# Top-2 routing of the first batch in two pieces: an mLSTM, MoE and dense layer kernel on one core

## The chip, the cores and the metric

The kernel runs on one core of a Trainium2 chip. Its time is the device time of one execution in microseconds. Before the change the median of three runs is 506.29 us (506.05 to 507.14).

The core has five engines that run their own instruction queues in order: PE (TensorE, matmuls and transposes), DVE (VectorE), ACT (ScalarE), POOL (GpSimd) and SP (SyncE, which here only starts DMAs). They wait for each other by semaphores. SBUF is the working memory, and PSUM is the memory that PE writes to and that DVE and ACT can read and write.

## The reference

Three layers stand one behind the other, all in float32. The first is an mLSTM over 2 batches, 8 heads, 768 positions and 40 values a head. The second sends each of the 1536 tokens to two of eight experts. The third is dense with a cosine gate.

```python
# mLSTM, for each position t
m_new = np.maximum(f_gate[:, :, t] + m, i_gate[:, :, t])
C = f_stab * C + i_stab * outer(vt, kt);  n = f_stab * n + i_stab * kt
y[:, :, t] = sigmoid(o_gate[:, :, t]) * (C @ qt) / max(abs(n @ qt), 1)
# mixture of experts, x has 1536 rows of 320
logits = x @ w_gate
noisy_logits = logits + np.log1p(np.exp(x @ w_noise)) * noise
top2 = np.argpartition(-noisy_logits, 2, axis=1)[:, :2]
top2_w = softmax of the two noisy logits
out[mask] += top2_w[mask, k, None] * (np.maximum(x[mask] @ w1[e], 0.0) @ w2[e])
# dense layer
h = x @ w_in;  out = (h * np.cos(h)) @ w_out
```

## The kernel before

**Attention steps.** The mLSTM is computed in chunks of 128 positions: chunks 0 to 5 are the first batch (b = 0), 6 to 11 the second. `att_step(n)` (L857) is one step of a pipeline over the chunks. In step n, `mm_out(n)` computes the output of chunk n on PE, while `mm_s(n + 2)` makes the scores of a later chunk, `mk_w` (ACT's exponentials with POOL's masks) makes its decay weights, and `mk_p(n + 1)` (DVE, into `ppt`) multiplies the two. `mk_e` makes the exponentials for the state (`get`), `mk_q` the scaled queries (`qtt`), `mm_state` and `mk_state` the state. `mk_y(n)` (L326) turns the output of chunk n into the rows x(n): an Abs on ACT and four instructions on DVE, the last of which is L338 and writes `xt`. `tanh_o` (L151) prepares the output gates of two chunks in a tile `ogt`.

**Router.** x(n) is transposed on PE by `rt_a(n)` (L352, copy on ACT into `xTt`) and multiplied with the router's weights by `rt_b(n)` (L361, copy on ACT into `Lt`, called Lt(n) below); both run one step later, in step n + 1. When all six chunks of a batch are there, `router_a0` and `router_a1` make the noisy logits and their top 2 (`r_mx`, `r_ix`), `router_a2` the one-hot rows `r_os`, `router_b` the place of every token in its expert's list (`pp` and `jj` hold place and block), `router_b1` and `router_b2` one-hot matrices of these (`r_am`, `r_bm`), and `router_c` on PE and `router_d` on DVE the list of tokens, by which POOL's indirect DMAs gather rows. `router_a3` and `router_a4` make the softmax of the two weights, which is used only when the expert outputs are combined.

**What sets the order.** Instructions stand in each engine's queue in the order in which the code calls them. Around the fixed body of `att_step`, tables insert further calls: `inner[n, w]` inside mm_out(n) after head pair w, `mid[n]` before rt_b(n - 1), `fill[n]` before mk_y(n), and `put(n, ...)` at the end of step n. After attention, `expert_step` runs 64 times (two steps begin inside attention), and `put(k, ...)` with the same k adds work to expert step k. Experts' weights are split by ACT and POOL or DVE into `wh` and `wl`.

**Buffers.** A tile gets one buffer of a ring when it is made, and the first instruction that writes to it waits until all instructions on the buffer's former tile are done. PSUM has rings of four (`psA`), three (`psS`) and one (`psM`). rt_b, router_b and router_c use the single `psM`. mm_state(n) and mm_out(n) each take a tile of `psS` in every step with a state, and rt_a takes its tile from there in steps 7 and 9, otherwise from `psM`. In batch 0, `pp` and `jj` lie in SBUF; in batch 1 they lie in the PSUM tile of router_b.

**Around the change.** In step 6 (L928 to L931) ACT changes its function table, because Ln is not in the one used until then, and the whole top 2 of batch 0 is made; tanh_o(5) stands at the end of step 5, the last place where the old table holds. router_a4(0) stands at the end of step 9, in spare columns of mm_out(9)'s tile.

Of the kernel before, what the change touches and what calls it, by code (L numbers as in the profile page):

```python
# [14 lines left out]
U32 = mybir.dt.uint32  # L15
AF = mybir.ActivationFunctionType
OP = mybir.AluOpType
# [5 lines left out]
NC = S // C  # L23
DM = H * D
E = 8
# [16 lines left out]
def tile_mlstm_moe_moe2(ctx, tc, qk, kv, og, gt, wcat, noise, wm1, wm2, cst, out):  # L42
    nc = tc.nc
    V, A, G, T, Y = nc.vector, nc.scalar, nc.gpsimd, nc.tensor, nc.sync
# [13 lines left out]
    def psS():  # L58
        return ps.tile([128, 512], FT, name="pS", tag="S", bufs=3)

    def psM():
        return ps.tile([128, 512], FT, name="pM", tag="M", bufs=1)
# [65 lines left out]
    for i in range(NB):  # L128
        t = ap_.tile([128, 3, NH, C], FT, name=f"qk{i}")
# [4 lines left out]
    for i in range(2):  # L134
        t = ap_.tile([128, H, 64], FT, name=f"kb{i}")
        G.memset(t, 0.0)
        KBS.append(t)
    for i in range(2):
        t = ap_.tile([128, NH, 82], FT, name=f"st{i}")
# [14 lines left out]
    L = [{} for _ in range(2 * NC)]  # L154
# [189 lines left out]
    nz = cp.tile([128, B * NC, E], FT, name="nz")  # L344
    R = [dict() for _ in range(B)]

    def cols(x, n, k):

        c0 = min(128 * k, DM - 128)
        return x[:n, c0:c0 + 128]  # L350

    def rt_a(n, ps_=None):  # L352
        b, c = divmod(n, NC)
        d = L[n]
        p = (ps_ or psM)()
        for k in range(3):
            T.transpose(p[:, 128 * k:128 * k + 128], cols(d["x"], 128, k), ident)
        d["xT"] = ap_.tile([128, 3, 128], FT, name="xTt", bufs=2)
        A.activation(d["xT"], p[:, :KW].rearrange("p (k t) -> p k t", t=128), AF.Copy)

    def rt_b(n, ps_=None):  # L361
        b, c = divmod(n, NC)
        d = L[n]
        p = (ps_ or psM)()
        for k in range(3):
            T.matmul(p[:, :128], d["xT"][:, k, :], wc[:, k:k + 1, :].to_broadcast([128, 8, 16]),  # L366
                     start=(k == 0), stop=(k == 2))
        if c == 0:
            R[b]["L"] = mp.tile([128, NC, 16], FT, name="Lt", bufs=1)
        A.activation(R[b]["L"][:, c, :], p[:, :16], AF.Copy)  # L370
# [20 lines left out]
    def rsm(shape, name, dt=FT):  # L391
        return mp.tile(shape, dt, name=name, tag=name, bufs=1)
# [2 lines left out]
    rb = rsm([128, B, E], "r_rb", BF)  # L395


    def router_a0(b):
        r = R[b]
        q = r["q"] = psM()  # L400
        t = r["t"] = q[:, 0:48].rearrange("p (c e) -> p c e", e=E)
        A.activation(t, r["L"][:, :, 8:16], AF.Abs)
        A.activation(t, t, AF.Exp, scale=-1.0)
        A.activation(t, t, AF.Ln, bias=1.0)

    def router_a1(b):
        r = R[b]
        t, z, lg = r["t"], r["L"][:, :, 8:16], r["L"][:, :, 0:8]
        V.scalar_tensor_tensor(out=t, in0=z, scalar=0.0, in1=t, op0=OP.max, op1=OP.add)
        V.tensor_tensor(out=t, in0=t, in1=nz[:, b * NC:(b + 1) * NC, :], op=OP.mult)  # L410
        ts = rsm([128, NC, E], "r_t")
        V.tensor_tensor(out=ts, in0=t, in1=lg, op=OP.add)
        mx = rsm([128, NC, 8], "r_mx")
        ix = rsm([128, NC, 8], "r_ix", U32)
        for c in range(NC):
            V.max(out=mx[:, c, :], in_=ts[:, c, :])
        for c in range(NC):
            V.max_index(out=ix[:, c, :], in_max=mx[:, c, :], in_values=ts[:, c, :])
        r["mx"], r["ix"] = mx, ix

    def router_a2(b):
        r = R[b]
# [17 lines left out]
    def router_a4(b, p=None):  # L440
        w = R[b]["w"]
        p = psM() if p is None else p
        e, t = p[:, 352:358], p[:, 360:366]
        A.activation(e, w[:, 1], AF.Exp)
        V.tensor_scalar(t, e, 1.0, 1e-9, op0=OP.add, op1=OP.add)
        V.reciprocal(w[:, 0], t)
        V.tensor_tensor(out=w[:, 1], in0=e, in1=w[:, 0], op=OP.mult)

    def router_b(b):

        r = R[b]
        q = r["q"] = psM()
        v = q[:, 384:384 + NC * E + E]
        T.matmul(v, tri, os_.rearrange("p c e -> p (c e)"), start=True, stop=False)
        T.matmul(v, ones, rb[:, b:b + 1, :].to_broadcast([128, NC + 1, E]), start=False, stop=False)
        for c in range(NC):
            T.matmul(v[:, (c + 1) * E:], ones, os_[:, c:c + 1, :].to_broadcast([128, NC - c, E]),
                     start=False, stop=(c == NC - 1))
        rk = q[:, 0:96].rearrange("p (k c e) -> p k c e", k=2, e=E)
        V.tensor_tensor(out=rk, in0=v[:, 0:NC * E].rearrange("p (c e) -> p c e", e=E)[:, None]  # L460
                        .to_broadcast([128, 2, NC, E]), in1=r["oh"], op=OP.mult)
        rr, y = (q[:, 440 + 12 * i:452 + 12 * i].rearrange("p (k c) -> p k c", c=NC) for i in range(2))
        V.tensor_reduce(rr, rk, axis=AX.X, op=OP.add)
        V.tensor_scalar(y, rr, -63.75, MAGIC7, op0=OP.add, op1=OP.add)
        js = rsm([128, 2, NC], "r_jj")
        jj, pp = ((q[:, 464 + 12 * i:476 + 12 * i].rearrange("p (k c) -> p k c", c=NC) for i in range(2)) if b else
                  (js, rsm([128, 2, NC], "r_pp")))
        V.tensor_scalar(js, y, MAGIC7, 1.0 / C, op0=OP.subtract, op1=OP.mult)
        V.scalar_tensor_tensor(out=pp, in0=js, scalar=-float(C), in1=rr, op0=OP.mult, op1=OP.add)
        if b:  # L470
            V.tensor_scalar(jj, y, MAGIC7, 1.0 / C, op0=OP.subtract, op1=OP.mult)
        r["pp"], r["jj"], r["rr"], r["tot"] = pp, jj, rr, v[:, NC * E:]
        if not b:
            router_p(b)
            router_s(q)

    def router_p(b):
        r = R[b]
        pos = r["pos"] = rsm([128, 2, NC], f"r_pos{b}", U32)
        V.tensor_scalar(pos, r["rr"], float(ROWS - 1 if b else ROW1[0] - 1), None, op0=OP.min)  # L480
        fl = rsm([128, E], "r_fl")
        V.tensor_tensor(out=fl, in0=r["tot"], in1=lims[b], op=OP.is_gt)
        V.tensor_reduce(flag[:, b:b + 1], fl, axis=AX.X, op=OP.max)

    def router_s(q):

        so, t = q[:, 128:136], q[:, 136:144]
        V.tensor_reduce(so, os_[:, 0:NC].rearrange("p c e -> p e c"), axis=AX.X, op=OP.add)
        V.tensor_tensor(out=t, in0=so, in1=joint, op=OP.mult)
        V.tensor_tensor(out=rb[:, 1], in0=t, in1=row1, op=OP.add)  # L490
# [366 lines left out]
    def att_step(n):  # L857
# [11 lines left out]
        def between(w):  # L869
            if n + 2 in ROWS64:  # L870
                if w == 1:
                    rt_a(n - 1)
                    mk_w(n + 2, (0,), False)
            elif w < NH - 2:
                mm_s(n + 2, (w + 1,))
            elif w == NH - 2:
                rt_a(n - 1, psS if n in (7, 9) else None)
            for f, a in inner.pop((n, w), []):
                f(*a)
# [6 lines left out]
        if n:  # L886
            rt_b(n - 1)
# [27 lines left out]
    at, pre, mid, fill, inner = {}, {}, {}, {}, {}  # L915

    def put(k, fn, *a):
        at.setdefault(k, []).append((fn, a))
# [1 line left out]
    def step(k):  # L920
        expert_step(*divmod(k, 8))

    for i in range(1, NC):
        put(i, tanh_o, i)
    for i in range(8):
        put((6, 7, 7, 8, 10, 10, 10, 11)[i], load_w, 0, i, 1)
    put(11, load_w, 1, 0, 2)
    mid[6] = [(A.preload_act_table_set, ("natural_log_exp_and_others",))]  # L928
    fill[6] = [(router_a0, (0,))]
    put(6, router_a1, 0)  # L930
    put(6, router_a2, 0)  # L931
    mid[7] = [(mk_w, (9, (0,), False))]
    fill[7] = [(mk_w, (9, (1,), False)), (mk_m, (9, 0, 1)), (router_b, (0,))]
    put(7, router_a3, 0)
    put(7, router_b1, 0, 0)
# [4 lines left out]
    inner[9, 1] = [(mk_w, (11, (0,), False))]  # L940
    mid[9] = [(mk_w, (11, (1,), False))]
    fill[9] = [(mk_m, (11, 0, 1))]
    put(9, lambda: router_a4(0, L[9]["po"]))
    put(10, split, 0)
    put(10, split, 1)
    inner[11, 0] = [(prep_slot, (0, 0, psA))]
# [6 lines left out]
    for n in range(2 * NC):  # L953
        att_step(n)
        for f, a in at.pop(n, []):
            f(*a)
    rt_a(2 * NC - 1)
    step(1)
    rt_b(2 * NC - 1)
    router_a0(1)  # L960
    router_a1(1)
    att.close()
    wp = ctx.enter_context(tc.tile_pool(name="wp", bufs=1, reuse_waits="tile"))

# [13 lines left out]
    put(7, router_d, 1)  # L978
    put(9, router_a3, 1)
    put(12, router_a4, 1)  # L980
    for i in range(4):
        put(7 + i // 2, gather, 2, i)
        put((13, 14, 15, 15)[i], prep_slot, 2, i, (psA, psM)[i % 2])
# [23 lines left out]
    for f in range(12):  # L1007
        k = 18 + (15 * f) // 4
# [10 lines left out]
    for q in range(3):  # L1019
        for i in range(3):  # L1020
            c = 3 * q + 3 + i
# [25 lines left out]
    with tc.If(over > 0):  # L1047
        WD = [dr.tile([S, E], FT, name=f"wd{b}") for b in range(B)]
        for b in range(B):
            r = R[b]  # L1050
# [6 lines left out]
        for b in range(B):  # L1057
            with tc.For_i(0, NC, 1) as it:
# [4 lines left out]
                p = psM()  # L1063
# [6 lines left out]
                for e in range(E):  # L1070
                    acc = psA()
                    for f in range(8):
                        w = mp.tile([128, FW], FT, name="wr", tag="wh", bufs=4)
                        Y.dma_start(w, wm1[e, :, f, :])
                        p = psS()
                        for k in range(3):
                            r = slice(64 * (k == 2), 128)
# [6 lines left out]
                                           in1=x2[:, :DM], op0=OP.mult, op1=OP.add)  # L1084
                d = {}
# [3 lines left out]
                for f in range(16):  # L1089
                    wh, wl = W2[f // 4][:, 0, f % 4, :], W2[f // 4][:, 1, f % 4, :]  # L1090
                    p = psS()
# [6 lines left out]
                t = mp.tile([128, DM], FT, name="yt", tag="yt", bufs=3)  # L1098
# [81 lines left out]
```

## Time and profile before

| | |
|---|---|
| median of the runs | 506.29 us |
| the profiled execution | 505.76 us |
| its span (first to last instruction) | 504.0 us |
| PE busy | 481.1 us (95%) |
| DVE busy | 353.2 us (70%) |
| ACT busy | 325.6 us (65%) |
| POOL busy | 273.1 us (54%) |
| granted TensorE clock | 0.998 of full speed |

The profile is one execution. The busy time of an engine says how full it is over the whole span; what a step waits for is read from the engines' timelines, where a row carries in brackets the idle time of the engine just before it and the instruction that ended it. Attention steps 5 to 11 take about 42 to 85 us of the span, and the expert steps follow up to about 280 us.

### The profile page before, as it was taken

The numbers are of one execution on the slowest core, as the hardware profiler recorded it, in microseconds if no ns is written. First come the engines' busy times: TensorE is split into PE (matmuls) and PEld (weight loads), VectorE is DVE, ScalarE is ACT, GpSimd is POOL, SyncE is SP. The second block draws the span as 40 slices with busy tenths as digits, with TensorE's granted clock in tenths as the row PEclk, the third lists the DMA queues.
The fourth block names the chain that finished last, engine by engine and source line by source line (L and its number), as shares of the span: only waits on it lengthen the run. The fifth ranks groups of instructions, "written<-read, shape, count | busy, mean of one in ns | idle before, by whom it ended". The sixth has DMA issues, their size and how long they took to land.

```text
span 504.0 us, 9162 instructions
## 1 busy us (share of the span) xinstructions
PE 481.1 (95%) x3295; PEld 466.0 (92%) x3295; DVE 353.2 (70%) x749; ACT 325.6 (65%) x691; POOL 273.1 (54%) x228
## 2 busy tenths in 40 slices
PE   5999889999999999999999989899999999999995
PEld 4998888989999999999999988899999999999995
DVE  4565697874577777787667588589756755787772
ACT  3787856655454545545553765678787787787772
POOL 4654665877558684968587786363364357200000
PEclk9999999999999999999999999999999999999999
DMA  6989754964739274645657373310020012001001
GB/s 200 299 286 295 236 180 144 322 211 152 294 128 322 103 260 176 257 182 188 257 166 263 117 284 100 105 52 1 0 92 29 0 35 84 2 2 39 1 2 45
DMA packets 25429, 74.47 MB, mean 148 GB/s; under 512 B 3840, under 2 KB 11456, under 8 KB 25376
## 3 DMA queue, kind: packets, MB, share of 16 engines
q1 hardware_dynamic: 22784, 65.20, 37.1%
q0 software_dynamic: 2592, 8.61, 5.7%
q8 instruction: 28, 0.46, 0.4%
q14 instruction: 25, 0.20, 0.1%
HBM read 64.57 MB, written 9.22 MB: 146 GB/s over the span
## 4 chain that ended last, share of the span: by engine, by line
PE 79%; DVE 9%; ACT 3%; issue 3%; DMA 2%; POOL 1%; SPq 1%; ACTq 0%; DVEq 0%; POOLq 0%
PE pS L606 34%; PE pA L615 10%; PE pA L611 10%; PE pA L612 10%; PE pS L321 3%; PE pM L567 2%; DMA wraw<-wm 2%; PE pA L262 1%; PE pA L623 1%; PE pA L624 1%; PE pS L317 1%; PE pM L366 1%; PE pA L253 1%; DVE c_t L729 1%; POOL xgt L558 1%
## 5 line engine op out<-in xcount | busy, mean ns | idle before, releaser
L599 POOL TENSOR_TENSOR wl<-wraw,wh 128x704 fp32r<-128x704 f32 x70 | 125.2, 1801 | 59.8 <-ACT wh L597 53.1
L661 DVE SCALAR_TENSOR_TENSOR hb<-pS,hb 128x384 fp32r<-128x384 f32 (+2 forms) x128 | 45.8, 390 | 45.2 <-ACT hb L658 44.5
L597 ACT ACTIVATE wh<-wraw 128x704 fp32r<-128x704 f32 x80 | 62.8, 786 | 15.8 <-PE pA L623 9.3
L606 PE MATMUL pS<-xh,wh 128*128 128x448 f32 (+1 forms) x240 | 69.3, 343 | 0.5 <-ACT xh L569 0.5
L606 PE MATMUL pS<-xh,w 128*128 128x384 f32 x288 | 66.3, 339 | 1.5 <-DVE m_t L770 1.5
L606 PE MATMUL pS<-xh,wl 128*128 128x448 f32 (+1 forms) x240 | 65.9, 329 | 1.0 <-POOL wl L599 1.0
L611 PE MATMUL pA<-wh,hb 128*128 128x320 f32 x208 | 62.3, 309 | 0.0
L612 PE MATMUL pA<-wl,hb 128*128 128x320 f32 x208 | 62.2, 309 | 0.0
L755 ACT ACTIVATE m_t<-pS,magic 128x384 f32<-128x384 f32 x64 | 37.1, 579 | 27.7 <-PE pS L606 27.2
L658 ACT ACTIVATE hb<-pS 128x448 fp32r<-128x448 f32 (+1 forms) x80 | 37.7, 471 | 26.7 <-PE pS L606 19.2
L606 PEld LDWEIGHTS pS<-xh,w 128*128 128x128 f32 x288 | 50.1, 189 | 2.9 <-DVE m_t L770 2.9
L770 DVE SCALAR_TENSOR_TENSOR m_t<-m_t,pS 128x384 f32<-128x384 f32 x64 | 35.4, 553 | 16.9 <-ACT m_t L769 16.3
L615 PE MATMUL pA<-wh,hb 128*128 128x320 f32 x208 | 44.0, 311 | 2.8 <-DVE hb L661 2.6
L606 PEld LDWEIGHTS pS<-xh,wl 128*128 128x128 f32 x240 | 42.8, 189 | 3.6 <-POOL wl L599 1.4
L606 PEld LDWEIGHTS pS<-xh,wh 128*128 128x128 f32 x240 | 40.5, 189 | 1.6 <-ACT xh L569 0.6
L776 POOL TENSOR_TENSOR wl<-m_t,wh 128x384 fp32r<-128x384 f32 x25 | 25.5, 1019 | 30.2 <-ACT wh L774 21.1
L756 DVE TENSOR_SCALAR m_t<-m_t 128x384 f32<-128x384 f32 x64 | 23.1, 361 | 26.4 <-ACT m_t L755 26.2
L606 PE MATMUL pS<-xl,wh 128*128 128x448 f32 (+1 forms) x160 | 39.6, 328 | 0.0
L611 PEld LDWEIGHTS pA<-wh,hb 128*128 128x128 f32 x208 | 38.7, 186 | 0.6
L612 PEld LDWEIGHTS pA<-wl,hb 128*128 128x128 f32 x208 | 38.7, 186 | 0.5
L569 ACT ACTIVATE xh<-pM 128x384 fp32r<-128x384 f32 (+2 forms) x38 | 17.6, 462 | 30.5 <-PE pM L567 30.4
L757 DVE SCALAR_TENSOR_TENSOR m_t<-pS,m_t 128x384 f32<-128x384 f32 x64 | 35.7, 557 | 2.2
(217 smaller groups left out, 1226.7 us busy)
## 6 DMA issues: line engine op xcount, KB each, us to landing
wraw<-wm SPq DMA_DIRECT2D x36, 704.0 KB
raw<-wm SPq DMA_DIRECT2D x16, 704.0 KB
gb<-gd SPq DMA_DIRECT2D x10, 512.0 KB
kv<-kv SPq DMA_DIRECT2D x12, 324.0 KB
qk<-qk SPq DMA_DIRECT2D x24, 160.0 KB
yd<-yt SPq DMA_DIRECT2D x22, 160.0 KB
wraw<-wm SPq DMA_DIRECT2D x8, 352.0 KB
ogt<-og SPq DMA_DIRECT2D x6, 320.0 KB
```

Source lines behind the costliest of these rows:

```text
L597: A.activation(wh, raw[:, f, :], AF.Copy)
L599: eng.tensor_tensor(out=wl, in0=raw[:, f, :], in1=wh.bitcast(FT), op=OP.subtract)
L606: T.matmul(p[:, :n], w[:, 128 * k:128 * k + 128], x[:, m, :], start=(i == 0), stop=(i == 7))
L611: T.matmul(a[:n, :DM], hh[:, s], wh[:, KW:], start=first, stop=False)
L612: T.matmul(a[:n, :DM], hh[:, s], wl[:, KW:], start=False, stop=False)
L615: T.matmul(a[:n, :DM], hl[:, s], wh[:, KW:], start=False, stop=last)
L658: A.activation(hh[:, :n], p[:, :n], AF.Relu)
L661: V.scalar_tensor_tensor(out=hb[:, o:o + z - a], in0=p[:, a:z], scalar=0.0, in1=hh[:, a:z].bitcast(FT), op0=OP.max, op1=OP.subtract)
L755: A.activation(t, m["p"], AF.Identity, bias=magic, scale=0.5 / PI)
L757: V.scalar_tensor_tensor(out=t, in0=m["p"], scalar=0.5 / PI, in1=t, op0=OP.mult, op1=OP.subtract)
L770: V.scalar_tensor_tensor(out=s, in0=s, scalar=1.0, in1=m["p"], op0=OP.subtract, op1=OP.mult)
L776: eng.tensor_tensor(out=m["hl"], in0=m["t"], in1=m["hh"].bitcast(FT), op=OP.subtract)
```

## The change

The top 2 of batch 0 is now made in two pieces. Chunks 0 to 4 go through router_a0 and router_a1 in step 5, and chunk 5 alone in step 6, followed by router_a2 as before. router_a0 now includes the three DVE instructions that were the beginning of router_a1, so these stand where `fill` stands, ahead of mk_y. The scratch columns are taken from the tile of the last rt_b instead of a new `psM` tile. The table load and tanh_o(5) move into mm_out(5) behind head pair 1. `pp` of batch 0 moves from an SBUF tile to columns 384 to 395 of the PSUM tile of rt_a(6) (`L[NC]["pt"]`). router_a4(0) moves to expert step 13 with a `psM` tile.

```diff
     def rt_a(n, ps_=None):
-        p = (ps_ or psM)()
+        p = d["pt"] = (ps_ or psM)()
     def rt_b(n, ps_=None):
-        p = (ps_ or psM)()
+        p = d["pl"] = (ps_ or psM)()
-    def router_a0(b):
+    def router_a0(b, c0, c1):
         r = R[b]
-        q = r["q"] = psM()
-        t = r["t"] = q[:, 0:48].rearrange("p (c e) -> p c e", e=E)
-        A.activation(t, r["L"][:, :, 8:16], AF.Abs)
+        p = r["q"] = L[b * NC + c1 - 1]["pl"]
+        t = p[:, 128 + c0 * E:128 + c1 * E].rearrange("p (c e) -> p c e", e=E)
+        A.activation(t, r["L"][:, c0:c1, 8:16], AF.Abs)
         A.activation(t, t, AF.Exp, scale=-1.0)
         A.activation(t, t, AF.Ln, bias=1.0)
-    def router_a1(b):
+        z, lg = r["L"][:, c0:c1, 8:16], r["L"][:, c0:c1, 0:8]
         V.scalar_tensor_tensor(out=t, in0=z, scalar=0.0, in1=t, op0=OP.max, op1=OP.add)
...
+    def router_a1(b, c0, c1):
...
-        for c in range(NC):
+        for c in range(c0, c1):
             V.max(out=mx[:, c, :], in_=ts[:, c, :])
-        for c in range(NC):
+        for c in range(c0, c1):
             V.max_index(out=ix[:, c, :], in_max=mx[:, c, :], in_values=ts[:, c, :])
...
-                  (js, rsm([128, 2, NC], "r_pp")))
+                  (js, L[NC]["pt"][:, 384:396].rearrange("p (k c) -> p k c", c=NC)))
...
-    for i in range(1, NC):
+    for i in range(1, NC - 1):
         put(i, tanh_o, i)
...
-    mid[6] = [(A.preload_act_table_set, ("natural_log_exp_and_others",))]
-    fill[6] = [(router_a0, (0,))]
-    put(6, router_a1, 0)
+    inner[5, 1] = [(tanh_o, (5,)), (A.preload_act_table_set, ("natural_log_exp_and_others",))]
+    fill[5] = [(router_a0, (0, 0, 5))]
+    put(5, router_a1, 0, 0, 5)
+    fill[6] = [(router_a0, (0, 5, 6))]
+    put(6, router_a1, 0, 5, 6)
     put(6, router_a2, 0)
...
-    put(9, lambda: router_a4(0, L[9]["po"]))
...
+    put(13, router_a4, 0)
```

On ACT, in step 5, before (Lt_354 of pM_652 is Lt(4), pS_618 the tile of mm_out(5), ogt_526 the gates of tanh_o(5)):

```order
L205 ACTIVATE wt_631<-gb_522,tok_86 128x128 x4
L370 ACTIVATE Lt_354<-pM_652 128x16
L332 ACTIVATE pS_618<-pS_618 128x8
L205 ACTIVATE wt_631<-gb_522,tok_86 128x128 x4
L152 ACTIVATE ogt_526<-ogt_526 128x640
L225 ACTIVATE get_680<-gb_522 64x512 x2
```

and now:

```order
L152 ACTIVATE ogt_526<-ogt_526 128x640
L882 ACT_TABLE_LOAD
L370 ACTIVATE Lt_354<-pM_654 128x16
L402 ACTIVATE pM_654<-Lt_354 128x40
L403 ACTIVATE pM_654<-pM_654 128x40
L404 ACTIVATE pM_654<-pM_654 128x40
L332 ACTIVATE pS_618<-pS_618 128x8
L205 ACTIVATE wt_631<-gb_522,tok_86 128x128 x4
```

The tanh and the table load now stand ahead of Lt(4), and three more activations between Lt(4) and the Abs of mk_y(5).

On DVE, from mk_y(5) on, before (pS_618 is the tile of mm_out(5), pS_684 that of mm_state(6)):

```order
L333 TENSOR_SCALAR pS_618<-pS_618 128x8
L334 RECIPROCAL pS_618<-pS_618 128x8
L335 SCALAR_TENSOR_TENSOR ogt_283<-ogt_283,pS_618 128x320
L338 SCALAR_TENSOR_TENSOR xt_670<-pS_618,ogt_283 128x320
L302 COPY st0_102<-pS_684 40x4x41 x2
```

and now:

```order
L406 SCALAR_TENSOR_TENSOR pM_654<-Lt_354,pM_654 128x40
L407 TENSOR_TENSOR pM_654<-pM_654,nz_108 128x40
L410 TENSOR_TENSOR r_t_673<-pM_654,Lt_354 128x40
L333 TENSOR_SCALAR pS_618<-pS_618 128x8
L334 RECIPROCAL pS_618<-pS_618 128x8
L335 SCALAR_TENSOR_TENSOR ogt_283<-ogt_283,pS_618 128x320
L338 SCALAR_TENSOR_TENSOR xt_679<-pS_618,ogt_283 128x320
L420 MAX r_mx_688<-r_t_673 128x8 x5
L422 MAX_INDEX r_ix_689<-r_mx_688,r_t_673 128x8 x5
L302 COPY st0_102<-pS_704 40x4x41 x2
```

Three instructions now stand ahead of mk_y(5), and ten behind it; in step 6 three stand ahead of mk_y(6) in the same way, and two of the twelve MAX and MAX_INDEX are left.

On PE, at the beginning of mm_out(8) in step 8, before, with the semaphores that an instruction waits for (pS_891 is the tile of mm_state(8), pS_899 that of mm_out(8)):

```order
L280 MATMUL pS_891<-kv_664,kb0_98 104x82 [waits DMAHW5_49,DVE_49,Pool_49]
L280 MATMUL pS_891<-kv_664,kb0_98 104x82 x3
L262 MATMUL pA_896<-qk1_93 128x128 [waits DMAHW7_49,DMAHW0_49,DVE_49]
L262 MATMUL pA_896<-qk1_93 128x128
L317 MATMUL pS_899<-st1_104,qtt_835 128x82 [waits Pool_49]
L321 MATMUL pS_899<-kv_664,ppt_832 128x2x41
L321 MATMUL pS_899<-kv_664,ppt_832 128x2x41 [waits DVE_49]
```

and now (pS_903 is the tile of mm_out(8)):

```order
L280 MATMUL pS_895<-kv_666,kb0_98 104x82 [waits DMAHW5_49,DVE_49,Pool_49]
L280 MATMUL pS_895<-kv_666,kb0_98 104x82 x3
L262 MATMUL pA_900<-qk1_93 128x128 [waits DMAHW7_49,DMAHW0_49,DVE_49]
L262 MATMUL pA_900<-qk1_93 128x128
L317 MATMUL pS_903<-st1_104,qtt_840 128x82 [waits DVE_49,Activation_49,Pool_49]
L321 MATMUL pS_903<-kv_666,ppt_837 128x2x41 x2
```

The first matmul of mm_out(8) now also waits for DVE and ACT: by the counts of the semaphores these are the last instruction of mk_y(7) (L338, which reads the tile of mm_out(7)) and its Abs (L332). In the same way mm_out(9) now waits for the second router_b1 of batch 0.

## Rows read from the trace of the kernel before

**Rows 1.** Timeline of PE, steps 6 to 11: start us, duration us, engine, line, instruction, [idle before, releaser].

```profile
49.33 0.52 PE L357 MATMUL pM<-ci,xt 128*128 128x128 f32 x3 [0.33 <-DVE xt L338]
...
51.73 0.94 PE L366 MATMUL pM<-wc,xTt 128*128 128x128 f32 x6
...
59.33 0.91 PE L366 MATMUL pM<-wc,xTt 128*128 128x128 f32 x6 [1.16 <-DVE r_os L432]
60.50 0.18 PE L454 MATMUL pM<-r_os,tri 128*128 128x56 bf16 x1 [0.27 <-ACT Lt L370]
...
61.97 0.35 PE L317 MATMUL pS<-st,qtt 128*128 128x82 f32 x2
...
70.73 0.47 PE L517 MATMUL pM<-r_bm,r_am 128*128 128x32 f16 x12 [1.31 <-DVE r_bm L508]
...
79.00 0.94 PE L366 MATMUL pM<-wc,xTt 128*128 128x128 f32 x6 [0.16 <-ACT xTt L359]
80.52 0.42 PE L317 MATMUL pS<-st,qtt 128*128 128x82 f32 x2 [0.59 <-DVE pS L333]
```

**Rows 2.** Timeline of ACT, steps 5 and 6.

```profile
44.62 1.26 ACT L205 ACTIVATE wt<-gb,tok 128x128 f32<-128x128 f32 x4
47.43 0.18 ACT L370 ACTIVATE Lt<-pM 128x16 f32<-128x16 f32 x1 [1.55 <-PE pM L366]
...
47.57 1.27 ACT L205 ACTIVATE wt<-gb,tok 128x128 f32<-128x128 f32 x4
48.74 0.72 ACT L152 ACTIVATE ogt<-ogt 128x640 f32<-128x640 f32 x1
...
52.46 1.28 ACT L885 ACT_TABLE_LOAD   x1
53.75 0.18 ACT L370 ACTIVATE Lt<-pM 128x16 f32<-128x16 f32 x1
...
54.44 0.20 ACT L404 ACTIVATE pM<-pM 128x48 f32<-128x48 f32 x1
```

**Rows 3.** Timeline of DVE, steps 5 to 7.

```profile
47.72 0.17 DVE L333 TENSOR_SCALAR pS<-pS 128x8 f32<-128x8 f32 x1 [2.57 <-ACT pS L332]
...
48.70 0.49 DVE L338 SCALAR_TENSOR_TENSOR xt<-pS,ogt 128x320 f32<-128x320 f32 x1
...
56.12 0.20 DVE L409 SCALAR_TENSOR_TENSOR pM<-Lt,pM 128x48 f32<-128x48 f32 x1
...
56.85 0.51 DVE L416 MAX8 r_mx<-r_t 128x8 f32<-128x8 f32 x6
...
58.97 0.21 DVE L432 TENSOR_TENSOR r_os<-pM,r_oh 128x48 bf16<-128x48 f32 x1
...
60.99 0.26 DVE L460 TENSOR_TENSOR pM<-pM,r_oh 128x96 f32<-128x96 f32 x1
...
63.97 0.49 DVE L338 SCALAR_TENSOR_TENSOR xt<-pS,ogt 128x320 f32<-128x320 f32 x1
```

**Rows 4.** Timeline of PE, router_b of batch 1, behind expert step 4.

```profile
94.62 0.20 PE L454 MATMUL pM<-r_os,tri 128*128 128x56 bf16 x1
```

**Rows 5.** Timeline of DVE, router_b and the first router_b1 of batch 1.

```profile
95.03 0.27 DVE L460 TENSOR_TENSOR pM<-pM,r_oh 128x96 f32<-128x96 f32 x1 [0.28 <-PE pM L457]
...
97.14 0.94 DVE L497 TENSOR_TENSOR r_am<-pM,cc 128x768 f16<-128x768 f32 x1
```

**Rows 6.** Groups of DVE, 60 to 75 us: line, instruction, count, busy us, mean ns, idle before.

```profile
L497 DVE TENSOR_TENSOR r_am<-r_pp,cc 128x768 f16<-128x768 f32 x2 | 3.4, 1710 | 0.0
```

**Rows 7.** Timeline of DVE, steps 9 and 10.

```profile
76.46 0.49 DVE L338 SCALAR_TENSOR_TENSOR xt<-pS,ogt 128x320 f32<-128x320 f32 x1
...
77.80 0.66 DVE L304 TENSOR_TENSOR st<-pS,st 40x164 f32<-40x164 f32 x2
...
79.70 0.68 DVE L239 TENSOR_TENSOR qtt<-qk,get 128x512 f32<-128x512 f32 x1
```

**Rows 8.** Timeline of PE, expert step 12.

```profile
109.84 0.49 PE L606 MATMUL pS<-xh,wl 128*128 128x240 f32 x2 [0.65 <-POOL wl L599]
```

More of the change, by code (lines that the diff above doesn't have):

```diff
@@ L395, in tile_mlstm_moe_moe2 @@
     rb = rsm([128, B, E], "r_rb", BF)
-    def router_a0(b):
+    def router_a0(b, c0, c1):
         r = R[b]
-        q = r["q"] = psM()
-        t = r["t"] = q[:, 0:48].rearrange("p (c e) -> p c e", e=E)
-        A.activation(t, r["L"][:, :, 8:16], AF.Abs)
+        p = r["q"] = L[b * NC + c1 - 1]["pl"]
+        t = p[:, 128 + c0 * E:128 + c1 * E].rearrange("p (c e) -> p c e", e=E)
+        A.activation(t, r["L"][:, c0:c1, 8:16], AF.Abs)
         A.activation(t, t, AF.Exp, scale=-1.0)
         A.activation(t, t, AF.Ln, bias=1.0)
-    def router_a1(b):
-        r = R[b]
[L408 to L414, printed above, removed]
-        for c in range(NC):
+        z, lg = r["L"][:, c0:c1, 8:16], r["L"][:, c0:c1, 0:8]
+        V.scalar_tensor_tensor(out=t, in0=z, scalar=0.0, in1=t, op0=OP.max, op1=OP.add)
+        V.tensor_tensor(out=t, in0=t, in1=nz[:, b * NC + c0:b * NC + c1, :], op=OP.mult)
+        if c0 == 0:
+            r["ts"] = rsm([128, NC, E], "r_t")
+        V.tensor_tensor(out=r["ts"][:, c0:c1], in0=t, in1=lg, op=OP.add)
+    def router_a1(b, c0, c1):
+        r = R[b]
+        ts = r["ts"]
+        if c0 == 0:
+            r["mx"] = rsm([128, NC, 8], "r_mx")
+            r["ix"] = rsm([128, NC, 8], "r_ix", U32)
+        mx, ix = r["mx"], r["ix"]
+        for c in range(c0, c1):
             V.max(out=mx[:, c, :], in_=ts[:, c, :])
-        for c in range(NC):
+        for c in range(c0, c1):
             V.max_index(out=ix[:, c, :], in_max=mx[:, c, :], in_values=ts[:, c, :])
-        r["mx"], r["ix"] = mx, ix
     def router_a2(b):
@@ L959, in tile_mlstm_moe_moe2 @@
     rt_b(2 * NC - 1)
-    router_a0(1)
-    router_a1(1)
+    router_a0(1, 0, NC)
+    router_a1(1, 0, NC)
     att.close()
```

## The prediction

> **What bounds the kernel now.** I read the timeline of PE first, because PE is busy nearly all the time and a gain or loss has to show as one of its few idle stretches. From attention step 5 to step 11 there are six that matter [rows 1]: 0.33 us before the transposes of x(5), 1.16 before rt_b(6), which waits for `r_os` (the end of router_a2), 0.27 for the copy Lt(6), 1.31 before router_c, which waits for `r_bm`, 0.16 before rt_b(9), and 0.59 before mm_out(11). Between them PE runs without a gap, so a delay put on it at one place travels until one of these idle stretches swallows it, and a wait taken away is worth its length only if nothing else is late there. Next I read ACT and DVE over the same stretch [rows 2, 3]. In step 6 ACT is the late one: its table load sits right before Lt(5) and the router's three activations. In step 5 ACT has 1.55 us of idle time before Lt(4). DVE is idle in most of step 5 and runs from step 6 to router_c with hardly a pause.
>
> There is one hand-over per step that has no slack. rt_b(4) on PE, then on ACT Lt(4) and the Abs of mk_y(5), then on DVE the four instructions of mk_y(5), then on PE rt_a(5) inside the next step. PE already waited 0.33 us for this chain [rows 1].
>
> **The change part by part.** *Step 5, ACT.* tanh_o(5) and the table load now stand behind the four exponentials that end at 44.62 + 1.26 = 45.88. Tanh takes 0.72 and started 0.10 before the end of the exponentials ahead of it (47.57 + 1.27 = 48.84 against 48.74), the load takes 1.28 [rows 2]: 45.88 - 0.10 + 0.72 + 1.28 = 47.78. Lt(4) began at 47.43, so of 2.00 us of moved work the idle time hides all but 0.35.
>
> *Step 5, router_a0 ahead of mk_y(5).* Lt(4) to the end of Ln takes 54.44 + 0.20 - 53.75 = 0.89 [rows 2]. The three DVE instructions that follow take 56.85 - 56.12 = 0.73, and mk_y takes 48.70 + 0.49 - 47.72 = 1.47 [rows 3]. DVE's queue is in order, so all of mk_y(5) waits: x(5) is ready at 47.78 + 0.89 + 0.73 + 1.47 = 50.87 instead of 49.19. rt_a(5) starts 1.68 us later, at 51.01, and all that is queued on PE behind it with it. This cost is not covered: PE was already waiting there. At best, with everything new on ACT hidden, it is 1.33.
>
> *Step 6.* What the piece takes from here is large for DVE (five of six MAX and MAX_INDEX, and ACT's table load and tanh), but it pays only the 1.16 us that PE waited at rt_b(6). PE would come to rt_b(6) at 59.33 - 1.16 + 1.68 = 59.85. `r_os` is ready sooner: rt_b(5) ends at 51.73 + 0.94 + 1.68 = 54.35, Lt(5) starts about 54.40; then 0.89 + 0.73 + 1.47 and the rest of the chain, 59.18 - 56.85 = 2.33, less five MAX (5/6 of 0.51), end at 59.4 even if I leave the gone MAX_INDEX in [rows 1, 3]. So the 1.16 us go entirely, and PE is 0.52 behind the old time.
>
> *Step 8, the new wait.* For batch 0, `pp` no longer lies in SBUF but in the PSUM tile of rt_a(6). That tile is one of three in its ring, and it is now held from step 7 until the second router_b1 in step 8. The tile of mm_out(8) therefore gets the buffer of mm_out(7), and its first matmul waits for mk_y(7) on DVE, as the order of PE shows. mk_y(7) stands behind the eleven instructions of router_b. In the old times: router_b's first matmul at 60.50, DVE's first instruction after it at 60.99, x(7) ready at 63.97 + 0.49 = 64.46; PE began mm_out(8) at 61.97 [rows 1, 3]. New: router_b's matmul at 59.85 + 1.17 = 61.02; 0.41 later DVE starts, as in batch 1 where it was idle (94.62 to 95.03) [rows 4, 5]; after 64.46 - 60.99 = 3.47 x(7) is ready, at 64.90. From x(5) to its transposes PE needed 0.14 [rows 1, 3], so mm_out(8) starts at 65.04. PE is there at 61.97 + 0.52 = 62.49. The wait is 2.55 us, and queued behind it are the rest of step 8's PE work, mm_state(9), mm_out(9) and router_c. No row of before shows this wait; its ends are 0 (if mk_y(7) were in time) and 3.47 + 0.41 + 0.14 less what PE has to do between router_b and mm_out(8), 61.97 - 60.50 = 1.47, which is the same 2.55. I take it in full.
>
> *Router_c.* PE was ready at 70.73 - 1.31 = 69.42 and will be at 69.42 + 0.52 + 2.55 = 72.49. DVE needed 70.73 - 64.46 = 6.27 from x(7) to router_c, so it is ready at 71.17 at its old speed. It should be faster: the two `r_am` builds took 1.71 on average with `pp` in SBUF, and 0.94 in batch 1 with `pp` in PSUM [rows 5, 6], which makes it 69.63. Either way PE is the later one, and DVE's saving buys only the 1.31 us. PE is 1.76 late here. mm_out(9), whose buffer now waits for the second `r_am` build, is covered: that build ends before `r_bm` does, while PE comes to mm_out(9) only shortly before router_c.
>
> *Step 9.* router_a4(0) leaves. It held DVE from x(9), at 76.46 + 0.49 = 76.95, to mk_state(10) at 77.80, 0.85 us, and ACT's Exp waited for x(9) with the exponentials of mk_e(11) queued behind it. Without it mk_q(11) is ready at 79.70 + 0.68 + 1.76 - 0.85 = 81.29 [rows 7]. PE comes to mm_out(11) at 80.52 - 0.59 - 0.16 + 1.76 = 81.53. Both waits, 0.75 in all, go.
>
> *Expert step 13.* One ACT and three DVE instructions. In step 9 they cost 0.85 in line; here PE has a step of finished work ahead of both engines, so the cost is between 0 and 0.85 and I take 0, since in this part PE waits little.
>
> *After that* PE's waits follow from work that PE itself released, the largest being 0.65 for POOL's weight split [rows 8], so I let the shift run through to the end. If POOL's chain there did not move with PE, up to 0.65 would come back.
>
> Sum: +1.68 - 1.16 + 2.55 - 1.31 - 0.16 - 0.59 = +1.01 us. The profiled execution took 505.76 us (span 504.0), so it would be 506.8; the median of the runs lies 0.53 above the profiled one, and on it the forecast is 506.29 + 1.01 = 507.3.
>
> **A rule weighed.** The load took 1.28 us and Lt(5) began 0.01 after its end [rows 2]. The Trainium skill, "ScalarE: Activation LUTs", section "What ACT_TABLE_LOAD costs", says that every switch to another set costs about 2.66 us, the load and as long again for a drain. The trace does not agree: 1.28 and no more stand between what was ahead of the load and what came behind it. By the page Lt(4) would come 1.38 later than in my sum, and the total would be +2.4.
>
> **The rivals.** *Faster: the shorter DVE run decides.* If mm_out(8) did not have to wait for x(7), PE would reach router_c at 69.94 with `r_bm` ready at 69.63: 1.68 - 1.16 - 1.31 - 0.75 = -1.54, or 504.8. It decides if x(7) is ready by 62.35. For it: DVE is late at both of the large waits that the change shortens. Against it: router_b stands ahead of mk_y(7) in DVE's queue and starts only after 61.0. Chance 0.07.
>
> *About the same: part is given back later.* If POOL's 0.65 us swallow their length, +0.36 remains, 506.7. For it: that wait ends on another engine. Against: that engine's gathers wait for indices that router_c of batch 1 makes, and PE issues that. Chance 0.20.
>
> *Slower by more: ACT in step 5 is later than I think.* This happens if the engine pauses about the load, or if tanh's gate tile, which is now wanted 3 us sooner (45.78 instead of 48.74), has not landed. A delay there goes straight into x(5), and from rt_a(5) to mm_out(8) nothing absorbs it. With 1.38 more, 508.7. Against: at the old place the load had no pause behind it. Chance 0.05.
>
> **How the numbers follow.** The forecast, +1.0 by two new PE waits against four old ones, has 0.68, with a range of its own of 506.9 to 507.9 (the lower end takes 1.33 for x(5), the upper adds most of the 0.85 of step 13). Together with the case of 506.7 and the edges of the others, 506.2 to 508.1 holds 8 in 10. A run of this kernel can tell 0.2%, about 1.0 us, from no change, and the forecast lies on that line: half of its 0.68, and all of 0.05, fall above 507.3. Faster 0.07, same 0.52, slower 0.41, with the edges rounded.
>
> **What would show it.** PE's rt_a(5) should wait about 2.0 us for xt; rt_b(6) should wait for no `r_os`; mm_out(8)'s first matmul (L317) should wait about 2.5 us for xt L338, the largest PE wait in the attention part; router_c (now L520) should wait for nothing; the `r_am` builds should take about 0.95 each; mm_out(11) should not wait. ACT's table load should stand at about 46.5 and take 1.28. I am wrong if the wait at mm_out(8) is under 1 us, if PE is early at router_c, or if the idle time of PE after expert step 2 differs by more than 0.3 us from before.

## The result, and the profile after

The changed kernel took 513.3 us (median of six runs, 512.11 to 513.77), the kernel before 506.72 beside it (six runs, 506.05 to 507.85). The ratio is 1.0125, with a 95% interval of 1.0107 to 1.0143. It is slower by 6.6 us; the prediction said 1.0, and its range ended at 508.1.

The profiled execution took 513.2 us, its span is 511.5. I look first at PE again. These are rows of its timeline from step 6 to expert step 12 (start us, duration us, engine, line, instruction, then the idle time before it and what ended it):

```profile
51.83 0.52 PE L357 MATMUL pM<-ci,xt 128*128 128x128 f32 x3 [1.92 <-DVE r_mx L420]
...
62.08 0.83 PE L366 MATMUL pM<-wc,xTt 128*128 128x128 f32 x6
63.19 0.19 PE L457 MATMUL pM<-r_os,tri 128*128 128x56 bf16 x1 [0.27 <-ACT Lt L370]
...
67.26 0.64 PE L317 MATMUL pS<-st,qtt 128*128 128x82 f32 x2 [2.44 <-DVE xt L338]
...
77.89 0.46 PE L520 MATMUL pM<-r_bm,r_am 128*128 128x32 f16 x12
...
85.99 0.94 PE L366 MATMUL pM<-wc,xTt 128*128 128x128 f32 x6
86.77 0.39 PE L317 MATMUL pS<-st,qtt 128*128 128x82 f32 x2
...
116.09 0.49 PE L609 MATMUL pS<-xh,wl 128*128 128x240 f32 x2 [0.72 <-POOL wl L602]
```

They answer to [rows 1] and [rows 8], and as a list of waits they are what was forecast. rt_a(5) waits 1.92 us. (The row names `r_mx`, but x(5) ended just before it: the last row of step 5 below.) rt_b(6), router_c, rt_b(9) and mm_out(11) wait for nothing. mm_out(8) waits 2.44 us for x(7). POOL's wait of 0.65 is now 0.72.

The chain in step 5 also ran as it was worked out. ACT first, then DVE:

```profile
46.69 0.73 ACT L152 ACTIVATE ogt<-ogt 128x640 f32<-128x640 f32 x1
47.43 1.28 ACT L882 ACT_TABLE_LOAD   x1
48.73 0.18 ACT L370 ACTIVATE Lt<-pM 128x16 f32<-128x16 f32 x1
```

```profile
49.62 0.20 DVE L406 SCALAR_TENSOR_TENSOR pM<-Lt,pM 128x40 f32<-128x40 f32 x1 [3.58 <-ACT pM L404]
...
51.19 0.49 DVE L338 SCALAR_TENSOR_TENSOR xt<-pS,ogt 128x320 f32<-128x320 f32 x1
...
67.03 0.95 DVE L500 TENSOR_TENSOR r_am<-pS,cc 128x768 f16<-128x768 f32 x1
...
69.79 0.95 DVE L500 TENSOR_TENSOR r_am<-pS,cc 128x768 f16<-128x768 f32 x1
```

The load takes 1.28 us and Lt(4) starts 0.02 after it, and the two `r_am` builds take 0.95 each [rows 2, 3, 5, 6]. So why 6.6 us? The list of waits doesn't show it; the granted clock does. Here are windows of PE (from:to, length, PE busy and instructions, granted clock, DMA share, GB/s):

```profile
46.00:50.00 4.00, 3.90 (x42) 1.00 1.03 319
50.00:52.00 2.00, 0.17 (x2) 1.00 0.73 216
52.00:54.00 2.00, 2.00 (x23) 0.92 0.35 129
54.00:56.00 2.00, 2.00 (x14) 0.50 0.46 160
56.00:58.00 2.00, 2.00 (x17) 0.73 0.96 353
...
66.00:68.00 2.00, 0.74 (x4) 0.83 0.30 118
68.00:70.00 2.00, 2.00 (x11) 0.50 0.83 223
...
72.00:74.00 2.00, 2.00 (x11) 0.50 0.00 0
74.00:76.00 2.00, 2.00 (x20) 0.96 0.23 45
76.00:80.00 4.00, 4.00 (x47) 1.00 0.51 141
```

Behind each of the two new waits TensorE's clock falls to 0.50, its lower level of 1.2 GHz, and comes back some microseconds later. This is one execution, but the mean granted clock over the span was 0.986 to 0.989 in all six runs, and 0.998 in the profiled execution of the kernel before. PE counts as fully busy at 0.50, while the same work takes longer. Four matmuls of the same kind in and after the second low stretch:

```profile
68.55 1.14 PE L262 MATMUL pA<-qk 128*128 128x128 f32 x4
...
76.29 0.65 PE L262 MATMUL pA<-qk 128*128 128x128 f32 x4
```

A last part comes late and without any wait or low clock. From the wait of 0.47 us for `xh` to the wait of 1.72 for `hb` PE is never idle; the kernel before took 298.81 - 118.81 = 180.00 us for that, the changed one 306.27 - 125.02 = 181.25. The groups of PE in this stretch (count, busy us, mean ns, idle), of before and then of after:

```profile
L606 PE MATMUL pS<-xh,wl 128*128 128x448 f32 x144 | 44.5, 363 | 0.0
L606 PE MATMUL pS<-xl,wh 128*128 128x448 f32 x96 | 27.1, 364 | 0.0
```

```profile
L609 PE MATMUL pS<-xh,wl 128*128 128x448 f32 x144 | 45.0, 367 | 0.0
L609 PE MATMUL pS<-xl,wh 128*128 128x448 f32 x96 | 27.6, 368 | 0.0
```

The same instructions take 4 ns longer each, 1.0 of the 1.25 us together.

### The profile page after: what moved, and what is told of

Read it like the earlier page. It is cut to its first block, busy times and chain, and to the rows that moved or that the text cites. A ratio compares the mean times of both kernels' runs of the same rounds, so it can differ in the third digit from the quotient of the medians.

```text
span 511.5 us, 9173 instructions
## 1 busy us (share of the span) xinstructions
PE 487.4 (95%) x3295; PEld 471.5 (92%) x3295; DVE 352.5 (69%) x752; ACT 326.1 (64%) x694; POOL 271.8 (53%) x228
## 4 chain that ended last, share of the span: by engine, by line
PE 82%; DVE 6%; ACT 3%; issue 3%; DMA 2%; POOL 1%; SPq 1%; ACTq 0%; DVEq 0%; POOLq 0%
PE pS L609 34%; PE pA L618 10%; PE pA L614 10%; PE pA L615 10%; PE pS L321 4%; PE pA L262 3%; PE pM L570 2%; DMA wraw<-wm 2%; PE pS L317 2%; PE pM L366 1%; PE pA L627 1%; PE pA L626 1%; PE pA L253 1%; PE pS L280 1%; DVE c_t L732 1%
```

## The experiments

Theory 1: the waits cost what the prediction said, and the rest is the clock that falls behind them. Theory 2: the low clock costs little, and the time goes in the order on DVE or in the expert part. The start of the kernel differs between executions (rt_a(4) starts at 45.23 us in e1_filled and at 43.36 in e5_fill_fit, whose code is the same up to there; eight matmuls at about 11 us take 1.96 us in the first and 1.08 in the second), so I compare the distance from rt_a(4) to the wait for `xh`: 118.81 - 43.61 = 75.20 us before, 125.02 - 44.52 = 80.50 after.

**Keeping TensorE at work in the two waits.** These lines were added to the changed kernel. The two counts stand in brackets behind each run's name; here they are those of e5_fill_fit.

```diff
+    def spin(n, k):
+        for _ in range(k):
+            T.matmul(L[n]["pst"][:, 328:456], ident, ident, start=True, stop=True)
...
+                    if n == 6:
+                        spin(6, 8)
                     rt_a(n - 1)
...
+        if n == 8:
+            spin(8, 10)
         mm_out(n, between if n else None)
```

e1_filled, (15, 19). 

> The changed kernel with TensorE kept at work in its two new waits: 15 matmuls of the identity with itself (128x128) stand ahead of rt_a(5) and 19 ahead of mm_out(8), into 128 spare columns of the state tiles; nothing reads them. What is waited for (x(5), x(7)) is untouched. Theory 1 (the waits cost about what the prediction said, +1.0 us in all, and the rest of the +6.6 us is TensorE's clock, which fell to its lower level after each of them): granted clock 1.00 in every 2 us stretch from 46 to 76 us, no idle time over 0.5 us before rt_a(5) and mm_out(8), and 507.0 to 508.5 us. Theory 2 (the clock's fall costs little, the time goes in waits and in the expert part, through the order on VectorE or through router_a4(0) at expert step 13): 512 to 513.5 us, whatever the clock shows.

Measured: 511.41 us, clock 1.00 in all windows, the stretch 78.51. The time lies between the two theories' numbers, because the fillers were sized wrongly: each of these float32 matmuls is two instructions (x20 for ten in the row of e5_fill_fit below), so they ran on after the awaited x was there. Hence:

e5_fill_fit, (8, 10). 

> e1_filled with the number of matmuls fitted to the waits: one 128x128 matmul of the identity took 0.225 us there (two instructions of 0.112), so 8 ahead of rt_a(5) (1.80 us for a wait of 1.92) and 10 ahead of mm_out(8) (2.25 us for 2.44). In e1_filled they ran 1.46 and 1.80 us past the waits' ends, 3.26 of the 3.31 us by which it was longer than the kernel before between rt_a(4) and the wait for xh. Theory 1: clock 1.00 throughout; that stretch (75.20 us in the kernel before, 80.50 in the changed one) is 75.2 to 76.3; 507.5 to 509 us, the upper half if the 1.25 us of the expert part stays. Theory 2: the stretch stays above 79 us, 511 to 513.

Measured: 508.1 us (ratio to before 1.0032, 1.0022 to 1.0043), 5.2 below the changed kernel, with work added. The stretch is 75.66 us. PE in the second wait, and its windows there:

```profile
61.90 2.40 PE L312 MATMUL pS<-ci 128*128 128x128 f32 x20
64.51 0.42 PE L321 MATMUL pS<-st,qtt 128*128 128x82 f32 x2 [0.21 <-DVE xt L342]
```

```profile
66.00:68.00 2.00, 2.00 (x21) 1.00 0.92 297
68.00:70.00 2.00, 2.00 (x21) 1.00 0.34 105
```

PE gets to mm_out(8)'s work no sooner than in the changed kernel (4.07 us after router_b's first matmul in both), but does what follows at full speed. Theory 2 falls here.

e11_fill_half, (3, 5). 

> e5_fill_fit with about half the filling matmuls: 3 ahead of rt_a(5) and 5 ahead of mm_out(8), so that TensorE stays idle for about 1.25 and 1.3 us, the length of the waits (1.16 and 1.31 us) after which the clock stayed at 1.00 in the kernel before. Theory 1: the clock holds: 507.5 to 509 us, as e5_fill_fit. Rival: any idle added here lowers it, the filling only covers it: a stretch at 0.50 after at least one of the two, 510 to 513 us.

Measured: 508.77 us (507.36 to 511.64 in nine runs). In the profiled run PE is idle for 1.22 and 1.33 us, and the clock stays at 1.00:

```profile
51.22 0.52 PE L361 MATMUL pM<-ci,xt 128*128 128x128 f32 x3 [1.22 <-DVE r_mx L424]
65.07 0.42 PE L321 MATMUL pS<-st,qtt 128*128 128x82 f32 x2 [1.33 <-DVE xt L342]
```

Its stretch is 75.68. Three of the nine runs took 511 us or more. Their mean granted clocks are 0.992, 0.995 and, in the slowest, 0.996, the same as in the profiled run of 509.13; the other six have 0.993 to 0.999. So a low clock doesn't explain the slowest, and what made these three slow stays open. The profiled run itself loses time in the expert part: PE has two waits there, 0.19 us at 295.85 and 0.48 at 297.85, that the other traces don't have.

**One wait at a time.** e2_pp_sbuf removes the second wait:

```diff
-                  (js, L[NC]["pt"][:, 384:396].rearrange("p (k c) -> p k c", c=NC)))
+                  (js, rsm([128, 2, NC], "r_pp")))
```

> The changed kernel with pp of the first batch back in SBUF (r_pp), so that rt_a(6)'s PSUM buffer comes free early: only the wait of rt_a(5) is left. Theory 1: no wait at mm_out(8), clock low only in one stretch near 54 to 57 us; sum against the kernel before +1.6 (wait for x(5)) +1.7 (its low clock) -1.2 (rt_b(6)) -0.7 (router_a4) and 0 to -1.3 at router_c: 506 to 508 us. Theory 2: the gain against the changed kernel is the 2.5 us of the wait alone or less: 510 to 512 us.

Measured: 508.75 us, the stretch 77.76. rt_a(5) waits 1.92, mm_out(8) doesn't wait, and router_c waits 1.32 again. Above theory 1's 508, since the low clock lasted longer than behind the same wait in the changed kernel:

```profile
52.00:54.00 2.00, 2.00 (x15) 0.50 0.32 85
...
56.00:58.00 2.00, 2.00 (x12) 0.50 0.91 340
58.00:60.00 2.00, 2.00 (x17) 0.84 0.01 4
```

From rt_a(5) to router_b's first matmul e2_pp_sbuf took 64.08 - 51.12 = 12.96 us, the changed kernel 11.36, e5_fill_fit at full clock 9.78: the low clock costs 3.18 us in one execution and 1.58 in another.

e3_piece_late removes the first wait instead:

```diff
+        if b == 0 and c0 == 0:
+            t = rsm([128, 5, E], "r_t0")
-    fill[5] = [(router_a0, (0, 0, 5))]
+    put(5, router_a0, 0, 0, 5)
```

> The changed kernel with the first piece of the router (chunks 0 to 4) issued behind mk_y(5) instead of ahead of it, its scratch t in SBUF so that rt_a(5)'s PSUM buffer does not wait for it; pp stays in PSUM: only the wait of mm_out(8) is left. Theory 1: rt_a(5) waits 0.3 to 0.9 us, the clock stays at 1.00 there and falls once, after mm_out(8): +0.3 -1.2 +2.5 +3.4 -1.3 -0.7 = +3.0 against the kernel before, 509 to 510.5 us. Theory 2: gain of the first wait alone, 1.6 us or less: 511.5 to 513 us.

Measured: 509.08 us (506.39 to 511.57 in twelve runs). rt_a(5) waits 0.73 and mm_out(8) 2.44, and the clock is at 0.50 once, from 66 us on. The stretch is 76.14, +0.94, in the profiled run of 507.82 us. The wide spread fits a low clock whose length differs from run to run: the mean granted clock is 0.985 in the slowest run and 0.998 in the one of 506.71 us. At 0.998, as in the kernel before, that run has no room for a low stretch like the one traced, though its code has the same wait.

e4_both makes both edits. 

> Both at once: pp in SBUF and the first piece behind mk_y(5) with its scratch in SBUF; router in two pieces and router_a4(0) at expert step 13 stay. Theory 1: neither wait, clock 1.00 throughout, -1.2 (rt_b(6)) -0.7 (router_a4) and 0 to -1.3 (router_c), +0.3 (tanh and table load ahead of x(5)): 503.5 to 505.5 us, faster than the kernel before. Theory 2: 507 to 510 us, since the expert part's loss is still there.

Measured: 504.39 us, ratio 0.9961 (0.9948 to 0.9973): faster than the kernel before. The stretch is 73.45, with the clock at 1.00; against theory 1 it falls once, much later, behind the wait for `hb` (last section). Its PE waits from step 6 to 9:

```profile
50.03 0.52 PE L357 MATMUL pM<-ci,xt 128*128 128x128 f32 x3 [0.73 <-ACT r_t L405]
59.91 0.19 PE L459 MATMUL pM<-r_os,tri 128*128 128x56 bf16 x1 [0.27 <-ACT Lt L370]
70.15 0.47 PE L522 MATMUL pM<-r_bm,r_am 128*128 128x32 f16 x12 [1.32 <-DVE r_bm L513]
```

**Parts on the kernel before.** e8_before_a4 only moves router_a4(0):

```diff
-    put(9, lambda: router_a4(0, L[9]["po"]))
     put(12, router_a4, 1)
+    put(13, router_a4, 0)
```

> The kernel before with router_a4(0) alone moved from attention step 9 to expert step 13. Theory 1 and the prediction's last terms: the waits of 0.16 at 79.00 and 0.59 at 80.52 go, 505.6 to 506.0 us (at worst 506.4 where POOL's 0.65 swallows it). Theory 2 (expert step 13 pays for it): 507 us or more.

Measured: 505.6 us, ratio 0.9988 (0.9976 to 1.0). The waits at rt_b(9) and mm_out(11) are gone, and the stretch is 74.37, -0.83.

e9_before_pp_psum only moves `pp` into rt_a(6)'s tile, with a pad:

```diff
-        p = (ps_ or psM)()
+        p = d["pt"] = (ps_ or psM)()
...
-                  (js, rsm([128, 2, NC], "r_pp")))
+                  (js, L[NC]["pt"][:, 384:396].rearrange("p (k c) -> p k c", c=NC)))
...
+        if not b:
+            rsm([128, 2, NC], "r_pad")
```

> The kernel before with one thing changed: pp of the first batch in rt_a(6)'s PSUM tile, as in the changed kernel (a pad of 64 bytes keeps all later SBUF addresses). Theory 1: a new wait of 2.4 to 2.6 us at mm_out(8) for x(7), r_am builds of 0.95 us, no wait at router_c (-1.3), and after the wait a stretch at granted clock 0.50 that costs 1 to 3.4 us: 508.5 to 511 us. The prediction's way of counting (waits at their length, clock unchanged): +1.2, 507.9 us, and 1.00 throughout.

Measured: 509.02 us, ratio 1.005 (1.0034 to 1.0067). So this one edit makes the second wait and the fall:

```profile
65.27 0.42 PE L317 MATMUL pS<-st,qtt 128*128 128x82 f32 x2 [2.47 <-DVE xt L338]
```

```profile
66.00:68.00 2.00, 2.00 (x14) 0.63 0.83 240
68.00:70.00 2.00, 2.00 (x12) 0.51 0.53 203
70.00:72.00 2.00, 2.00 (x20) 1.00 0.08 8
```

**The 1.25 us of the expert part.** Without `r_pp` every SBUF tile allocated later lies 64 bytes lower. e6_pad is the changed kernel with the two pad lines above. 

> The changed kernel with an unused tile of 64 bytes a partition in r_pp's old place, so that every SBUF tile allocated after it (xh, xl, hb and the first raw weights among them) has the address that it has in the kernel before; the change had moved them by 64 bytes. Between the wait for xh and the wait for hb (no PE idle, clock 1.00) the kernel before took 180.00 us, the changed one 181.25, e1_filled with the changed one's addresses 181.22, e2_pp_sbuf with those of before 180.02. If the addresses set it: 180.0 here, and 511.5 to 512.3 us in all. If it is chance or the change's order: 181.2 and 513.3.

Measured: 511.82 us, and 179.95 us in that stretch (305.00 - 125.05). The matmul is back at its old time:

```profile
L611 PE MATMUL pS<-xl,wh 128*128 128x448 f32 x96 | 27.1, 363 | 0.0
```

e7_before_shift is the kernel before with the same pad beside `r_pp`, which moves those tiles 64 bytes up. 

> The kernel before with an unused tile of 64 bytes a partition behind r_jj, so that the later SBUF tiles stand 64 bytes higher; nothing else differs. If addresses set the pace of the expert part: 181.2 us between the wait for xh and the wait for hb (180.00 before), and 507.3 to 508 us. If not: 180.0 and 506.4.

Measured: 180.77 us in the stretch and 507.31 in all, ratio 1.0012 (1.0000 to 1.0024). The addresses set it, though not by the same amount in both directions: here only the second of the two groups is slower, and that of `xh` and `wl` stays at 364 ns. The other traces bear it out. The stretch is 179.95 to 180.02 us in all five with the old addresses (the kernel before, e2_pp_sbuf, e6_pad, e8_before_a4, e9_before_pp_psum) and 181.22 to 181.25 in three with those of the changed kernel (the changed kernel, e1_filled, e5_fill_fit). e11_fill_half, with these too, has 182.03, its two extra waits included. `r_t0` moves the tiles again: 180.44 in e3_piece_late, 180.00 and 180.01 in e4_both and e10_po7.

```profile
L608 PE MATMUL pS<-xl,wh 128*128 128x448 f32 x96 | 27.5, 367 | 0.0
```

**A version without either wait.** e10_po7 is e4_both with `pp` in PSUM, in a tile that nobody wants soon, and a pad of 64 bytes:

```diff
-                  (js, rsm([128, 2, NC], "r_pp")))
+                  (js, L[7]["po"][:, 352:364].rearrange("p (k c) -> p k c", c=NC)))
```

> e4_both with pp in PSUM after all, but in spare columns of mm_out(7)'s own tile, which the next product in that buffer wants only at mm_out(9) (a pad keeps e4_both's SBUF addresses). r_am builds fall from 1.35 and 2.11 to 0.95 us each, so r_bm ends some 1.5 us sooner and the wait of 1.32 at router_c goes; mm_out(9) may wait 0 to 0.4 for the second r_am. Theory 1: 1.3 less than e4_both up to the first expert's stages, of which POOL's wait for wl (0.72) may take 0.7 back: 503.0 to 504.2 us, clock 1.00. Rival: holding that buffer makes a wait at mm_out(9) of over 1.3 us: 504.4 or more.

Measured: 503.79 us (502.74 to 504.65), ratio 0.9939 (0.9924 to 0.9954), the stretch 72.52. The wait at router_c is 0.30, mm_out(9) doesn't wait, and the clock is 1.00 throughout:

```profile
70.31 0.47 PE L524 MATMUL pM<-r_bm,r_am 128*128 128x32 f16 x12 [0.30 <-ACT wt L205]
```

It is the fastest measured here, 3.05 us below the kernel before beside it (506.84). e4_both ran on another occasion, so the 0.6 us between those two is not certain.

## Why the prediction was wrong

Its steps, with what each was to add on PE's way. The landmarks are the starts of rt_a(4), rt_a(5), router_b, mm_out(8), router_c and rt_b(10): 43.36, 50.66, 60.44, 64.51, 71.88 and 84.38 us in e5_fill_fit, 43.61, 49.33, 60.50, 61.97, 70.73 and 84.19 in the kernel before. "At full clock" sets these two against each other, each from the landmark before; "clock" is what the changed kernel took beyond e5_fill_fit.

| step | predicted | at full clock | clock |
|---|---|---|---|
| x(5) late at rt_a(5) | +1.68 | 7.30 - 5.72 = +1.58 | |
| no wait at rt_b(6), to router_b | -1.16 | 9.78 - 11.17 = -1.39 | 11.36 - 9.78 = +1.58 |
| mm_out(8) waits for x(7) | +2.55 | 4.07 - 1.47 = +2.60 | |
| no wait at router_c | -1.31 | 7.37 - 8.76 = -1.39 | 10.63 - 7.37 = +3.26 |
| router_a4(0) out of step 9 | -0.75 | 12.50 - 13.46 = -0.96 | |
| sum | +1.01 | +0.44 | +4.84 |

The mechanism was right: both new waits stand where the prediction put them and have the lengths it worked out to 0.11 us, the four old ones are gone, and the rest of the sum is within 0.25 us a step. POOL's wait gave nothing back, expert step 13 took nothing, and the table load came without a pause, so none of the rivals happened.

The step that failed is the pricing of the two waits, "I take it in full" for mm_out(8) and "rt_a(5) starts 1.68 us later": it let a wait on PE cost its own length and nothing more, and took the matmuls behind it at the durations of [rows 1]. Those were measured at clock 1.00; these windows of the kernel before lie behind its waits of 1.16 us (rt_b(6)) and 1.31 (router_c):

```profile
60.00:62.00 2.00, 1.73 (x24) 1.00 0.82 268
70.00:72.00 2.00, 1.26 (x20) 1.00 0.00 0
```

The longest wait that PE has anywhere behind the first 10 us of the kernel before is this one, and the clock held behind it (timeline row, then windows):

```profile
298.81 0.56 PE L615 MATMUL pA<-wh,hb 128*128 128x320 f32 x2 [1.72 <-DVE hb L661]
```

```profile
298.00:300.00 2.00, 1.19 (x10) 1.00 0.22 62
300.00:302.00 2.00, 2.00 (x18) 1.00 0.17 54
```

Both new waits are longer than that, so no row showed what they do. The two ends that the prediction gave for mm_out(8) bound the wait and not its price, and the range lacked that room upwards. At half clock the work behind the two waits took 4.84 us more. None of the three signs came by which the prediction would have called itself wrong: the wait at mm_out(8) was 2.44 us, PE was not early at router_c, and PE's waits behind expert step 2 add up to 6.56 us against 6.39. All three look at waits, and none at the clock.

The Trainium skill, "TensorE: Matmul & The Clock Gate", section "Part 1: The HAM clock gate", has a table of two states of TensorE's clock, 1.2 GHz when it has been idle and 2.4 GHz when it has been busy. The trace agrees: 0.50 behind idle times of 1.92 and 2.44 us, and 1.00 where work filled them (e5_fill_fit).

The second step that failed is "I let the shift run through to the end". The shift grew by 1.25 us on the way, because taking `r_pp` out of SBUF moved the experts' operands by 64 bytes. The prediction counted what `pp` in PSUM gains on DVE and what its PSUM tile blocks, and not that the SBUF tiles behind it move.

Sum: +0.44 + 4.84 + 1.25 = 6.53 us, against 6.6 between the medians. The two profiled spans are 7.5 us apart, but 0.91 of that lies ahead of rt_a(4), where both kernels run the same code; the eight matmuls at about 11 us took 1.97 us in one execution and 1.08 in the other.

## What to carry to other kernels

A new wait on TensorE costs only its length as long as the clock holds: when a change adds one that is longer than the waits behind which the old trace shows it holding, add a second term for the work behind it at half speed, with a range that starts at nothing, and read the granted clock by windows, not only the list of waits. The same wait can be made harmless by shortening it, by moving what holds it (a piece of work one place later in a queue, a scratch in a buffer that nobody wants soon: e4_both, e10_po7), or even by useless matmuls in it. When a tile leaves SBUF, look at what slides into other addresses, and keep a pad of its size to tell the two effects apart.

## What the runs showed of the hardware

- The granted clock fell to 0.50 behind all seven PE waits of 1.92 to 2.47 us in these traces (two each in the changed kernel and e6_pad, one each in e2_pp_sbuf, e3_piece_late and e9_before_pp_psum), and behind none of 1.33 us or less from step 5 to 9. Behind the wait of 1.72 to 1.75 us for `hb`, which every kernel here has, it held in eleven traces and fell in two, e4_both and e8_before_a4: near that length it differs from execution to execution. By its mean clock of 0.998 it seems to have held behind 2.44 us too in the run of 506.71 us of e3_piece_late, of which there is no trace. In e4_both that fall cost nothing in the end, since PE's next two waits (0.32 and 0.91 us in the kernel before) are gone and the rest of the span is 502.2 - 297.37 = 204.83 us against 205.19:

```profile
297.37 0.68 PE L620 MATMUL pA<-wh,hb 128*128 128x320 f32 x2 [1.74 <-DVE hb L666]
```

```profile
298.00:300.00 2.00, 2.00 (x11) 0.50 0.32 85
```

- What the same wait costs in clock differs too: 1.58 us in the changed kernel and 3.18 in e2_pp_sbuf, both behind 1.92 us at rt_a(5). It fits the spread of e3_piece_late, 5 us between its runs, against 0.7 in e4_both. What sets the length stays open.
- The float32 matmuls with 448 columns of `xh` with `wl` and of `xl` with `wh` took 362 to 368 ns on average, by where the SBUF tiles allocated after `r_pp` lie; those of `xh` with `wh` took 379 to 381 wherever they lay. A shift of 64 bytes made 3 to 4 ns in one of the two groups or in both, and 0.8 to 1.25 us over the expert part. Whether the matmuls' own operands matter or a tile that another engine uses at that time, and by which rule of addresses, stays open.
- The two `r_am` builds on DVE took 1.31 and 2.11 us with `pp` in SBUF (kernel before) and 0.95 each with only `pp` moved to PSUM (e9_before_pp_psum). POOL's instruction L239, which ran beside the first build in both traces, went from 1.98 to 1.27 us. That fits the two engines holding each other up, which no run here tests by itself.
